# Queries and keys of the first batch entry: three rows to a partition, turned by products with the identity

## The chip, the cores and the metric

The kernel runs on one core of a Trainium2 chip. The metric is the device time of one launch in microseconds. The core has TensorE (PE; PEld is its loading of stationary operands), VectorE (DVE), ScalarE (ACT), GpSimd (POOL) and SyncE (SP), which issues all DMAs of this kernel. Each engine works through its own instructions in order.

## What is computed

Attention on q, k, v of shape (2, 8, 576, 64), followed by two feed-forward layers on the 1152 rows of 512. The change lies in the attention, of which this is the core:

```
q_d, k_d, v_d = means over groups of 4 rows            # 144 coarse rows
out_d   = softmax(scale * q_d @ k_d.T) @ v_d           # coarse attention
out_up  = each row of out_d repeated 4 times
scores  = scale * q @ k.T, masked to |i - j| < 4       # local attention
out     = out_up + softmax(scores) @ v
```

After it come a mixture of 8 experts, out = sum over e of P[:, e] * (relu(x @ w1[e]) @ w2[e]) with P from 8 rounds of row and column normalization, and softplus(x @ w_in) @ w_out.

## The kernel before

The attention is cut into eight units (`class Unit`): one unit is a pair of heads of one batch entry, and its `n` runs from 0 to 7, so units 0 to 3 are the first batch entry. A unit's q and k (576 rows of 64 values for each of two heads) are loaded by `load_qk` with four DMAs of 144 KB: queries in partitions 0 to 63, keys in 64 to 127; a partition holds row p of each of nine blocks of 64 rows. A DMA piece is one row, 256 bytes. Units 1 and 2 load into buffers of the expert weights (`qkw`), the others into one buffer `qk`.

`setup(g)`, called for g = 0, 1, 2, turns three of the nine blocks: three TensorE transposes of 128x128 write a PSUM bank `tb`, whose partitions are then the 64 values of head 0 and of head 1. From `tb` VectorE sums groups of four columns into `qkd` (L539), ScalarE copies the keys, scaled, into `kT` (L550), and the queries go to `fine`, one half by VectorE (L551), one by ScalarE (L552). After the third call VectorE scales the coarse queries into `flat` (L545). The layout of a bank is block, then query or key, then row.

`scores` makes four score blocks of a unit ("c" is the coarse one, 0 to 2 the local ones), the softmax runs on VectorE and ScalarE (small, sc, ex), `turn` transposes the weights (L609, L619), and `values` multiplies them with v (L630 coarse, L641 local; these write the lower and the upper 64 partitions in turn). `stir` (L479) issues products of the identity whose results nothing reads; they stand ahead of the scores and turns of units 0 to 3, and eight more at the very start. The values v come in `vw` and `vd`; GpSimd sums `vd` into `vs` (L559, L560). In the second half of the attention the first steps of the experts (L866, L954) are put between (`beside`), and expert weights are split into two parts (w1h, w1l, w2h, w2l, L274 to L314).

In the attention a scheduler at build time sets the order on each engine, from the dependencies and its own estimates; from the experts on, the order is written by hand (`Order`). At most eight DMAs are outstanding: each waits for the one eight places earlier.

Of the kernel before, what the change touches and what calls it, by code (L numbers as in the profile page):

```python
# [9 lines left out]
F32 = mybir.dt.float32  # L10
# [4 lines left out]
ALU = mybir.AluOpType  # L15
AX = mybir.AxisListType
# [4 lines left out]
def attention_moe_mlp(ctx: ExitStack, tc: tile.TileContext, q, k, v, w_gate, w1, w2, w_in, w_out, out):  # L21
    nc = tc.nc
    B, H, S, D = q.shape
# [3 lines left out]
    P = 128  # L27
    R = 4
    SD = S // R
    HC = SD // 2  # L30
    QT = 64
    NQ = S // QT
    NB = 3
    CT = SD // NB
    KW = QT + 2 * R
    KD = DM // P
    SCALE = 1.0 / float(D) ** 0.5
# [24 lines left out]
    rows = [ctx.enter_context(tc.tile_pool(name="rows0", bufs=len(TILES[0])))]  # L62
# [32 lines left out]
    ident = const.tile([P, P], F32, name="ident")  # L95
# [357 lines left out]
    ap = at.__enter__()  # L453
# [18 lines left out]
    fine = [ap.tile([P, NB, 2, QT], F32, bufs=1, name=f"fine{g}") for g in range(NB)]  # L472
# [11 lines left out]
    class Unit:  # L484
# [12 lines left out]
        def load_qk(self):  # L497
            b, h0 = self.b, 2 * self.u
            if self.n in (1, 2):
                qk = wp.tile([P, OPS, 2, P], F32R, tag="w1h" if self.n == 1 else "w1l", name="qkw").bitcast(F32)  # L500
                qk = qk.rearrange("p a k c -> p (a k c)")[:, : NQ * 2 * D]
                qk = qk.rearrange("p (t h d) -> p t h d", t=NQ, h=2)
            else:
                qk = ap.tile([P, NQ, 2, D], F32, tag="qk", bufs=1, name="qk")
            self.qk = qk
            for w, src in enumerate((q, k)):
                for hh in range(2):
                    nc.sync.dma_start(
                        qk[w * QT : (w + 1) * QT, :, hh], src[b, h0 + hh].rearrange("(t p) d -> p t d", p=QT)
                    )  # L510

        def load_v(self):
            b, h0 = self.b, 2 * self.u
# [11 lines left out]
        def setup(self, g):  # L525

            if g == 0:
                self.kT = ap.tile([P, NQ, QT], F32, tag="kT", name="kT")
                self.qkd = ap.tile([P, NQ, 2, QT // R], F32, tag="qkd", name="qkd")
            qkd = self.qkd  # L530
            tb = self.bank("tb", 1)
            tiles = slice(NB * g, NB * g + NB)
            for j in range(NB):
                nc.tensor.transpose(
                    tb[:, j * P : (j + 1) * P], self.qk[:, NB * g + j].rearrange("p h d -> p (h d)"), ident
                )
            tb = tb[:, : NB * P]
            tbv = tb.rearrange("x (t w p) -> x t w p", t=NB, w=2)
            nc.vector.tensor_reduce(  # L539
                qkd[:, tiles].rearrange("x t w g -> x (t w) g"),  # L540
                tb.rearrange("x (t g r) -> x t g r", g=QT // R, r=R), axis=AX.X, op=ALU.add,
            )
            for hh in range(2 if g == NB - 1 else 0):
                half = slice(hh * D, (hh + 1) * D)
                nc.vector.tensor_scalar(  # L545
                    self.flat[half, :, hh].rearrange("x i (j g) -> x i j g", j=NB),
                    qkd[half, :, 0].rearrange("x (i j) g -> x i j g", i=NB),
                    SCALE / (R * R), None, op0=ALU.mult,
                )
            nc.scalar.mul(self.kT[:, tiles], tbv[:, :, 1], SCALE)  # L550
            nc.vector.tensor_copy(fine[g][:D, :, 0], tbv[:D, :, 0])  # L551
            nc.scalar.copy(fine[g][D:, :, 1], tbv[D:, :, 0])  # L552
            if g:
                return
            vd = self.vd

            self.vs = vs = ap.tile([HC, 2, 2, D], F32, tag="vs", name="vs")
            for c in range(2):
                nc.gpsimd.tensor_tensor(vd[:, c, :, 0:2, :], vd[:, c, :, 0:2, :], vd[:, c, :, 2:4, :], op=ALU.add)  # L559
                nc.gpsimd.tensor_tensor(vs[:, c], vd[:, c, :, 0, :], vd[:, c, :, 1, :], op=ALU.add)  # L560
# [133 lines left out]
    def logits():  # L694
        lg = bank("y", "lg")
        lts = [
            lowp[0].tile([P, SUMS * P], U32, tag="cva", name="lts").bitcast(F32)[: 2 * E],
            pair("lts").rearrange("p a c -> p (a c)")[: 2 * E],
        ]

        def half(s, j):
            lt = bank("at", "lt")
            terms = [
                (i, w, kk, x[s]) for i, w in (((4, 1), (5, 2)), ((3, 0), (1, 1)))[j]
                for kk in range(2) for x in (xh, xl)
            ]
            for n, (i, w, kk, x) in enumerate(terms):
                nc.tensor.matmul(
                    lt[: 2 * E, : HALF[s]], wgs[:, w, kk, :], x[:, i, kk, :],
                    start=(n == 0), stop=(n == len(terms) - 1),  # L710
                )
            nc.scalar.copy(halves(s, lts[s])[j], lt[: 2 * E, : HALF[s]])

        def short(s, t):
            o = t * P - T0[s]
            nc.tensor.transpose(
                lg[:, 2 * t * E : 2 * (t + 1) * E], lts[s][:, o : o + P], ident[: 2 * E, : 2 * E]
            )

        def done():  # L720
            nc.vector.tensor_reduce(
                pr, lg[:, : 2 * NTT * E].rearrange("p (t w e) -> p t e w", w=2, e=E), axis=AX.X, op=ALU.add
            )
            nc.vector.tensor_reduce(m1, prf, axis=AX.X, op=ALU.max)

        return half, short, done
# [339 lines left out]
    for n in range(len(stream) + LAG + 1):  # L1066
        if n < len(stream):
            x, blk = stream[n]
            i, j = divmod(n, len(blocks))
# [24 lines left out]
        for lag, what in ((LAG, "turn"), (LAG + 1, "values")):  # L1094
            if 0 <= n - lag < len(stream):
                x, blk = stream[n - lag]
# [22 lines left out]
    half, short, done = logits()  # L1119
# [46 lines left out]
    with tc.manual_schedule(engines=engines):  # L1166
# [3 lines left out]
        for n in range(BESIDE, len(steps)):  # L1170
            if n == CV:
                converting.append(order_.add(conversions(), 2))
            e, g, s, p = steps[n]
# [9 lines left out]
            half = [i for i in range(len(ys)) if (i + 1) * P > HALF[s]]  # L1183
            half = half[1:] + half[:1] if HALF[s] % P else half
            tiles = half + [i for i in range(len(ys)) if i not in half]
# [55 lines left out]
```

## Time and profile before

| | us |
|---|---|
| median of 3 runs | 1068.11 (1066.86 to 1068.22) |
| profiled execution | 1065.88 |
| its span | 1064.0 |
| TensorE busy | 1044.2 (98%) |
| VectorE busy | 692.5 (65%) |
| ScalarE busy | 570.0 (54%) |
| GpSimd busy | 556.1 (52%) |

The profile covers one execution; its times count from the start of the span. Busy TensorE means that matmuls are in flight, not that it runs at its peak, and the stirring products count as busy. A row of the timeline merges like instructions that follow each other: start, time, engine, line, operation, output and inputs, count, and in brackets the idle time before it with what ended it. A float32 product that is not a transpose shows as two records.

### The profile page before, as it was taken

What the parts mean: (1) busy time and instruction counts of PE and PEld (TensorE: products, weight loads), DVE (VectorE), ACT (ScalarE), POOL (GpSimd) and SP (SyncE); (2) the same over time, 40 slices, a digit from 0 to 9 for tenths busy, and PEclk for the clock granted to TensorE, in tenths of its full rate; (3) what the DMA queues carried; (4) which work ended last, traced back from release to release, by engine and by line L of the source; (5) the groups of instructions that cost most, each with busy time, mean ns of one, the idle gap of its engine ahead of it and who ended that gap; (6) DMA issues with size and microseconds to landing.
All of it is one profiled execution on the core that took longest, in us unless ns stands there. A gap on an engine that the chain in (4) does not pass through costs nothing.

```text
span 1064.0 us, 17733 instructions
## 1 busy us (share of the span) xinstructions
PE 1044.2 (98%) x6417; PEld 925.7 (87%) x6417; DVE 692.5 (65%) x1416; ACT 570.0 (54%) x1479; POOL 556.1 (52%) x575
## 2 busy tenths in 40 slices
PE   7989999999999999999999999999999999999998
PEld 5778888898999989898998989899998999888897
DVE  4896666765656566566756665665664677876674
ACT  4887654435444444454444445444544667666664
POOL 3658433487556575555556666664574413222322
PEclk8999999999999999999999999999999999999999
DMA  9463201233333335243333333443334485533752
GB/s 175 131 136 84 85 21 41 61 94 114 95 115 90 99 94 154 80 128 114 117 114 94 101 108 94 118 126 100 119 99 140 147 295 211 217 149 129 262 202 80
DMA packets 135799, 131.22 MB, mean 123 GB/s; under 512 B 36000, under 2 KB 112032, under 8 KB 135712
## 3 DMA queue, kind: packets, MB, share of 16 engines
q1 hardware_dynamic: 135712, 130.10, 39.9%
q8 instruction: 50, 0.82, 0.3%
q14 instruction: 37, 0.30, 0.1%
HBM read 104.64 MB, written 25.43 MB: 122 GB/s over the span
## 4 chain that ended last, share of the span: by engine, by line
PE 83%; DVE 8%; ACT 5%; POOL 2%; DMA 1%; issue 1%; SPq 0%; ACTq 0%
PE yps L954 41%; PE m L866 37%; POOL ab L830 2%; DVE ab L833 1%; ACT one L828 1%; DVE ab L826 1%; PE sc L582 1%; DVE one L824 1%; DVE xl L439 1%; DVE c L885 1%; PE pv L641 1%; DMA raw<-in_moe_w 1%; ACT ab L815 1%; PE tp L619 1%; PE sc L569 1%
## 5 line engine op out<-in xcount | busy, mean ns | idle before, releaser
L866 PE MATMUL m<-xh,w1h 128*128 128x320 f32 (+1 forms) x1120 | 333.8, 298 | 3.5 <-ACT t L878 2.4
L866 PE MATMUL m<-xl,w1h 128*128 128x320 f32 (+1 forms) x1120 | 331.7, 296 | 1.1 <-DVE xl L439 1.1
L866 PE MATMUL m<-xh,w1l 128*128 128x320 f32 (+1 forms) x1120 | 331.6, 296 | 0.0
L866 PEld LDWEIGHTS m<-xh,w1h 128*128 128x128 f32 x1120 | 211.8, 189 | 20.1 <-ACT t L878 4.0
L866 PEld LDWEIGHTS m<-xl,w1h 128*128 128x128 f32 x1120 | 211.9, 189 | 14.4 <-DVE xl L439 1.5
L866 PEld LDWEIGHTS m<-xh,w1l 128*128 128x128 f32 x1120 | 211.8, 189 | 0.3 <-issue 0.2
L954 PE MATMUL yps<-w2h,hh 128*128 128x512 f32 x502 | 198.9, 396 | 0.0
L954 PE MATMUL yps<-w2l,hh 128*128 128x512 f32 x502 | 198.3, 395 | 0.0
L954 PE MATMUL yps<-w2h,hl 128*128 128x512 f32 x502 | 195.9, 390 | 0.0
L954 PE MATMUL yps<-w2h,h 128*128 128x512 f32 x436 | 152.8, 392 | 0.0
L293 POOL TENSOR_TENSOR w1l<-sums,w1h 128x512 fp32r<-128x512 f32 x72 | 99.5, 1394 | 90.9 <-ACT w1h L291 79.3
L885 DVE TENSOR_TENSOR c<-m,t 128x256 f32<-128x256 f32 (+1 forms) x160 | 72.8, 455 | 114.0 <-PE m L866 68.8
L314 POOL TENSOR_TENSOR w2l<-raw,w2h 128x512 fp32r<-128x512 f32 x72 | 98.8, 1391 | 60.0 <-ACT w2h L312 59.8
L803 ACT ACTIVATE hh<-c 128x256 fp32r<-128x256 f32 (+1 forms) x138 | 60.8, 444 | 127.7 <-DVE c L885 127.5
L830 POOL TENSOR_TENSOR ab<-one,ab 128x320 f32<-128x320 f32 (+1 forms) x64 | 55.3, 866 | 141.0 <-ACT one L828 140.9
L984 DVE SCALAR_TENSOR_TENSOR acc<-yps,pr,acc 128x512 f32<-128x512 f32 x117 | 87.2, 745 | 53.0 <-PE yps L954 52.4
L805 DVE SCALAR_TENSOR_TENSOR hl<-c,hh 128x256 fp32r<-128x256 f32 (+1 forms) x138 | 93.3, 679 | 31.7 <-ACT hh L803 30.1
L954 PEld LDWEIGHTS yps<-w2h,hl 128*128 128x128 f32 x502 | 94.4, 188 | 21.6 <-issue 0.2
L954 PEld LDWEIGHTS yps<-w2h,hh 128*128 128x128 f32 x502 | 94.7, 189 | 12.5 <-DVE small L589 0.2
L878 ACT COPY t<-m 128x256 f32<-128x256 f32 (+1 forms) x160 | 62.6, 398 | 77.9 <-PE m L866 77.7
L954 PEld LDWEIGHTS yps<-w2l,hh 128*128 128x128 f32 x502 | 94.8, 189 | 10.7
L954 PEld LDWEIGHTS yps<-w2h,h 128*128 128x128 f32 x436 | 82.1, 188 | 14.7
(141 smaller groups left out, 1647.2 us busy)
## 6 DMA issues: line engine op xcount, KB each, us to landing
raw<-in_moe_w SPq DMA_DIRECT2D x72, 256.0 KB
raw<-in_moe_w SPq DMA_DIRECT2D x36, 512.0 KB
w1h<-s_in SPq DMA_DIRECT2D x14, 896.0 KB
w1l<-s_in SPq DMA_DIRECT2D x14, 896.0 KB
raw<-in_moe_w_in SPq DMA_DIRECT2D x32, 256.0 KB
raw<-in_moe_w_out SPq DMA_DIRECT2D x16, 512.0 KB
w2l<-s_out SPq DMA_DIRECT2D x14, 512.0 KB
w2h<-s_out SPq DMA_DIRECT2D x14, 512.0 KB
```

The lines of the kernel that those rows point to most:

```text
L293: behind(chain, nc.gpsimd.tensor_tensor(lo[:, part], sums, hi[:, part].bitcast(F32), op=ALU.subtract))
L314: behind(chain, nc.gpsimd.tensor_tensor(lo[:, i], raw[:, i], hi[:, i].bitcast(F32), op=ALU.subtract))
L439: nc.vector.tensor_tensor(xl[s][:, i, kk], src, xh[s][:, i, kk].bitcast(F32), op=ALU.subtract)
L569: nc.tensor.matmul(sc[:rows, i * w : (i + 1) * w], self.flat[:, i].rearrange("x h q -> x (h q)"), self.qkd[:, :, 1], start=True, stop=True,)
L803: nc.scalar.activation(hh, c, AF.Relu)
L805: nc.vector.scalar_tensor_tensor(out=hl, in0=c, scalar=0.0, in1=hh.bitcast(F32), op0=ALU.max, op1=ALU.subtract)
L830: nc.gpsimd.tensor_tensor(ab, one, ab, op=ALU.subtract)
L866: nc.tensor.matmul(b[:, :h], x[:, i, kk, :], y[s][:, i, kk, :], start=(not more and n == 0), stop=(n == 5), skip_group_check=more,)
L878: nc.scalar.copy(t, b[:, :h])
L885: nc.vector.tensor_tensor(c, b[:, :h], t, op=ALU.add)
L954: nc.tensor.matmul(y, a[:, f, tok], b[:, f, :], start=(start and m == 0), stop=(stop and m == 5))
L984: nc.vector.scalar_tensor_tensor(out=acc[t], in0=y, scalar=pr[:, t, e : e + 1], in1=acc[t], op0=ALU.mult, op1=ALU.add,)
```

## The change

For units 0 to 3 (`thirds`) a partition now holds, in each third of a head's rows, three rows that follow each other (g, then p, then j), so a DMA piece is 768 bytes. Turning such a third by a transpose of whole blocks would leave the rows in the order j, p. So the turning of a third is six products of the loaded data (stationary, 64 columns: one head's row j) with the identity (moving, 128 columns): for each j one product for head 0, into partitions 0 to 63, and one for head 1, into 64 to 127, and each writes every third column of `tb`. A bank's layout is now query or key, then rows in order, for all units. Units 4 to 7 keep their loads and transposes, which write two pieces of 64 columns each. What reads `tb` changes its views, not its sizes; `qkd` is laid out by third, then query or key.

```diff
@@ -499,15 +499,22 @@
             if self.n in (1, 2):
                 qk = wp.tile([P, OPS, 2, P], F32R, tag="w1h" if self.n == 1 else "w1l", name="qkw").bitcast(F32)
                 qk = qk.rearrange("p a k c -> p (a k c)")[:, : NQ * 2 * D]
+            else:
+                qk = ap.tile([P, NQ * 2 * D], F32, tag="qk", bufs=1, name="qk")
+            self.thirds = self.n < 4
+            if self.thirds:
+                qk = qk.rearrange("p (g h j d) -> p g h j d", g=NB, h=2, j=NB)
+            else:
                 qk = qk.rearrange("p (t h d) -> p t h d", t=NQ, h=2)
-            else:
-                qk = ap.tile([P, NQ, 2, D], F32, tag="qk", bufs=1, name="qk")
             self.qk = qk
             for w, src in enumerate((q, k)):
                 for hh in range(2):
-                    nc.sync.dma_start(
-                        qk[w * QT : (w + 1) * QT, :, hh], src[b, h0 + hh].rearrange("(t p) d -> p t d", p=QT)
-                    )
+                    rows = src[b, h0 + hh]
+                    if self.thirds:
+                        rows = rows.rearrange("(g p j) d -> p g j d", g=NB, j=NB)
+                    else:
+                        rows = rows.rearrange("(t p) d -> p t d", p=QT)
+                    nc.sync.dma_start(qk[w * QT : (w + 1) * QT, :, hh], rows)
@@ -526,30 +533,35 @@
             if g == 0:
                 self.kT = ap.tile([P, NQ, QT], F32, tag="kT", name="kT")
-                self.qkd = ap.tile([P, NQ, 2, QT // R], F32, tag="qkd", name="qkd")
+                self.qkd = ap.tile([P, NB, 2, CT], F32, tag="qkd", name="qkd")
             qkd = self.qkd
             tb = self.bank("tb", 1)
             tiles = slice(NB * g, NB * g + NB)
+            tb = tb[:, : NB * P]
             for j in range(NB):
-                nc.tensor.transpose(
-                    tb[:, j * P : (j + 1) * P], self.qk[:, NB * g + j].rearrange("p h d -> p (h d)"), ident
-                )
-            tb = tb[:, : NB * P]
-            tbv = tb.rearrange("x (t w p) -> x t w p", t=NB, w=2)
+                if self.thirds:
+                    to = tb.rearrange("x (w p j) -> x w p j", w=2, j=NB)[:, :, :, j]
+                    for hh in range(2):
+                        nc.tensor.matmul(
+                            to[hh * D : (hh + 1) * D], self.qk[:, g, hh, j],
+                            ident.rearrange("k (w p) -> k w p", w=2), start=True, stop=True,
+                        )
+                else:
+                    to = tb.rearrange("x (w t p) -> x w t p", w=2, t=NB)[:, :, j]
+                    nc.tensor.transpose(to, self.qk[:, NB * g + j].rearrange("p h d -> p (h d)"), ident)
             nc.vector.tensor_reduce(
-                qkd[:, tiles].rearrange("x t w g -> x (t w) g"),
-                tb.rearrange("x (t g r) -> x t g r", g=QT // R, r=R), axis=AX.X, op=ALU.add,
+                qkd[:, g].rearrange("x w g -> x (w g)"),
+                tb.rearrange("x (g r) -> x g r", r=R), axis=AX.X, op=ALU.add,
             )
             for hh in range(2 if g == NB - 1 else 0):
                 half = slice(hh * D, (hh + 1) * D)
                 nc.vector.tensor_scalar(
-                    self.flat[half, :, hh].rearrange("x i (j g) -> x i j g", j=NB),
-                    qkd[half, :, 0].rearrange("x (i j) g -> x i j g", i=NB),
-                    SCALE / (R * R), None, op0=ALU.mult,
+                    self.flat[half, :, hh], qkd[half, :, 0], SCALE / (R * R), None, op0=ALU.mult,
                 )
-            nc.scalar.mul(self.kT[:, tiles], tbv[:, :, 1], SCALE)
-            nc.vector.tensor_copy(fine[g][:D, :, 0], tbv[:D, :, 0])
-            nc.scalar.copy(fine[g][D:, :, 1], tbv[D:, :, 0])
+            tbv = tb.rearrange("x (w t p) -> x w t p", w=2, p=QT)
+            nc.scalar.mul(self.kT[:, tiles], tbv[:, 1], SCALE)
+            nc.vector.tensor_copy(fine[g][:D, :, 0], tbv[:D, 0])
+            nc.scalar.copy(fine[g][D:, :, 1], tbv[D:, 0])
```

The scheduler also moves instructions. Line numbers of the changed kernel are 11 to 13 higher from here on (L534 becomes L545, L569 L581, L582 L594, L619 L631, L641 L653). On TensorE at the head, from the last mask product of the first scores (qk is unit 0's data and stands just before, qkw unit 1's), before:

```order
L576 MATMUL sc<-mask,identb 128x216
L534 MATMUL tb<-ident,qkw 128x128 x3
L582 MATMUL sc<-kT,fine_147 128x72 x3
L534 MATMUL tb<-ident,qkw 128x128 x3
L582 MATMUL sc<-kT,fine_148 128x72 x3
L479 LDWEIGHTS identb
L479 MATMUL tp<-identb 128x512
L569 MATMUL sc<-qkd,flat_150 96x144 x3
```

and in the changed kernel:

```order
L588 MATMUL sc<-mask,identb 128x216
L545 MATMUL tb<-ident,qkw 64x128 x6
L594 MATMUL sc<-kT,fine_147 128x72 x3
L545 MATMUL tb<-ident,qkw 64x128 x6
L581 MATMUL sc<-qkd,flat_150 96x144 x3
L594 MATMUL sc<-kT,fine_148 128x72 x3
L479 LDWEIGHTS identb
L479 MATMUL tp<-identb 128x512
```

The coarse scores of unit 0 (flat_150) moved ahead of its second local block and of a stirring product. On VectorE at the same place (flat_150 is unit 0's coarse queries; the copies fine_147 and fine_148 behind it are unit 1's), before:

```order
L545 TENSOR_SCALAR flat_150<-qkd 64x3x48 x2
L539 TENSOR_REDUCE qkd<-tb 128x96
L551 COPY fine_149<-tb 64x3x64
L551 COPY fine_147<-tb 64x3x64
L539 TENSOR_REDUCE qkd<-tb 128x96
L551 COPY fine_148<-tb 64x3x64
L589 TENSOR_REDUCE small<-sc 96x3
L589 TENSOR_REDUCE small<-sc 128x3 x2
```

and in the changed kernel:

```order
L558 TENSOR_SCALAR flat_150<-qkd 64x3x48 x2
L552 TENSOR_REDUCE qkd<-tb 128x96
L563 COPY fine_149<-tb 64x3x64
L563 COPY fine_147<-tb 64x3x64
L552 TENSOR_REDUCE qkd<-tb 128x96
L601 TENSOR_REDUCE small<-sc 96x3
L601 TENSOR_REDUCE small<-sc 128x3 x2
L563 COPY fine_148<-tb 64x3x64
```

The maxima of unit 0's scores (small) moved ahead of the copy for unit 1's second third. On TensorE where unit 2 (again qkw) is turned, before:

```order
L534 MATMUL tb<-ident,qkw 128x128 x5
L619 MATMUL tp<-ident,ex 72x128 x3
L479 LDWEIGHTS identb
L479 MATMUL sc<-identb 128x512
L576 LDWEIGHTS identb
L576 MATMUL sc<-mask,identb 128x216
L582 MATMUL sc<-kT,fine_148 128x72 x3
L534 MATMUL tb<-ident,qkw 128x128
L479 LDWEIGHTS identb
L479 MATMUL tp<-identb 128x512
L641 MATMUL pv<-et,vw 64x64 x6
```

and in the changed kernel:

```order
L545 MATMUL tb<-ident,qkw 64x128 x7
L631 MATMUL tp<-ident,ex 72x128
L653 MATMUL pv<-et,vw 64x64 x6
L631 MATMUL tp<-ident,ex 72x128 x2
L479 LDWEIGHTS identb
L479 MATMUL sc<-identb 128x512
L588 LDWEIGHTS identb
L588 MATMUL sc<-mask,identb 128x216
L594 MATMUL sc<-kT,fine_148 128x72 x3
L545 MATMUL tb<-ident,qkw 64x128 x5
```

The six transposes of the first two thirds became twelve products, split 7 and 5, and a block of values (pv) moved up between them.

## Rows read from the trace of the kernel before

**Rows 1.** The page's first line.

```profile
span 1064.0 us, 17733 instructions
```

**Rows 2.** Stretches: length, busy (count) PE PEld DVE ACT POOL, clock, DMA, GB/s.

```profile
13.70:16.70 3.00, 0.00 (x0) 0.00 (x0) 2.32 (x10) 2.71 (x19) 1.55 (x4) 0.93 1.37 138
16.70:23.10 6.40, 6.36 (x27) 5.01 (x28) 2.58 (x12) 2.69 (x11) 0.87 (x2) 0.50 1.17 173
23.10:34.60 11.50, 11.50 (x116) 9.15 (x115) 8.20 (x30) 8.87 (x40) 3.59 (x7) 1.00 0.56 144
34.60:46.20 11.60, 11.60 (x122) 9.14 (x120) 10.59 (x32) 11.35 (x51) 9.50 (x13) 1.00 0.51 119
46.20:60.00 13.80, 9.60 (x90) 7.78 (x90) 13.00 (x33) 9.94 (x39) 12.24 (x16) 0.90 0.83 183
60.00:75.00 15.00, 13.05 (x120) 10.59 (x119) 13.45 (x42) 12.59 (x54) 8.93 (x10) 0.98 0.46 127
75.00:140.00 65.00, 64.94 (x555) 55.58 (x554) 45.64 (x124) 46.38 (x164) 40.49 (x42) 1.00 0.30 78
140.00:1064.00 924.00, 917.37 (x5346) 822.50 (x5343) 590.91 (x1125) 470.81 (x1098) 472.20 (x461) 1.00 0.38 124
```

**Rows 3.** The chain of waits, 0 to 36 us: start, us, what.

```profile
5.58 4.03 DMA qkw<-in_k
...
12.46 0.35 DVE fine L551
12.82 0.62 DVE small L589
...
16.74 1.17 PE tp L609 x6
...
34.63 0.38 DVE small L589
```

**Rows 4.** Timeline of TensorE at the head.

```profile
5.33 1.16 PE L479 MATMUL sc<-identb 128*128 128x512 bf16 x3
6.50 1.18 PE L534 MATMUL tb<-ident,qk 128*128 128x128 f32 x9
7.51 0.35 PE L576 MATMUL sc<-mask,identb 128*128 128x216 bf16 x2
9.74 0.52 PE L534 MATMUL tb<-ident,qkw 128*128 128x128 f32 x3 [1.88 <-DMA qkw<-in_k]
...
16.74 1.17 PE L609 MATMUL tp<-ident,ex 96*72 96x96 f32 x6 [3.15 <-DVE ex L597]
```

**Rows 5.** Timeline of TensorE: ordinary float32 products, and what follows them.

```profile
27.65 0.57 PE L641 MATMUL pv<-et,vw 72*64 72x64 f32 x12
28.15 0.44 PE L609 MATMUL tp<-ident,ex 96*72 96x96 f32 x3
...
42.20 0.90 PE L569 MATMUL sc<-qkd,flat 128*96 128x144 f32 x6
43.03 0.72 PE L630 MATMUL pv<-etc,vs 72*64 72x144 f32 x8
43.67 0.52 PE L619 MATMUL tp<-ident,ex 128*72 128x128 f32 x3
```

**Rows 6.** Timeline of VectorE.

```profile
46.46 0.38 DVE L589 TENSOR_REDUCE small<-sc 128x3 f32<-128x216 f32 x1 [0.89 <-PE sc L582]
...
48.22 2.25 DVE L435 TENSOR_TENSOR xf<-xf 128x256 f32<-128x256 f32 x1
...
65.10 0.41 DVE L435 TENSOR_TENSOR x<-xf 128x256 f32<-128x256 f32 x1
```

**Rows 7.** Columns as in rows 2: first loads; a stretch of larger packets.

```profile
2.00:10.00 8.00, 6.10 (x25) 2.85 (x26) 2.52 (x7) 1.54 (x6) 4.67 (x16) 1.00 1.01 183
24.50:27.00 2.50, 2.50 (x23) 2.30 (x22) 1.70 (x6) 1.48 (x10) 0.00 (x0) 1.00 1.05 327
```

## Prediction, made before the changed kernel ran

> **What bounds the kernel now.** I read the page's span first [rows 1], then the busy times by stretch [rows 2], then the chain of waits over the first 36 us [rows 3], then the timelines of TensorE and VectorE at the places that the change touches [rows 4 to 6], and last the DMA rates [rows 7]. The profiled execution is 1065.88 us, 1064.0 us of it span and 1.88 us around it.
>
> From 75 us to the end TensorE is the bound: 64.94 of 65 us and then 917.37 of 924 us busy [rows 2]. The change touches nothing there, so what it does is the shift with which the work at 75 us arrives. [...] Up to 16.7 us the chain is made of latencies: issuing and landing of the loads of units 0 and 1 (the last one 4.03 us from issue to landing), then VectorE and ScalarE on the first softmax [rows 3]. TensorE waits 1.88 us for unit 1's keys, and 3.15 us for the first normalized scores [rows 4]. [...] From 34.6 to 46.2 us TensorE (11.60 of 11.60), ScalarE (11.35) and VectorE (10.59) are all full; from 46.2 to 75 us VectorE leads, and TensorE idles 4.2 + 1.95 = 6.15 us [rows 2].
>
> **What one unit's turning costs.** Nine transposes begin at 6.50 and the next instruction at 7.51: 0.112 us each [rows 4]. Now there are 18 ordinary float32 products, each with 64 stationary and 128 moving columns, in pairs that write the lower and upper half of the partitions. The nearest rows are L630: four products of 144 columns into such halves, shown as eight records, take 43.67 - 43.03 = 0.64 us [rows 5], 0.16 us each, by columns 0.142 us for 128. So a unit takes 18 x 0.142 = 2.56 us in place of 1.01: **+1.55 us**. From below: L569, 96 stationary columns, takes (43.03 - 42.20)/3 = 0.277 us for 144 columns [rows 5], 0.246 for 128; two exactly side by side cost 0.123 each, a unit +1.2 us. From above, as long as pairs overlap: L641, 64 columns, (28.15 - 27.65)/6 = 0.083 [rows 5], doubled 0.167, a unit +2.0 us. I take L630, the form nearest to the new one. No row has an output that writes every third column; its price is a rival below.
>
> The trace has a float32 product at 0.246 us for 128 columns against a transpose at 0.112 [rows 4, 5]: 2.2 times. [...]
>
> **The head, up to 16.7 us.** The gain is the load. Eight DMAs of 144 KB carry units 0 and 1, 1.18 MB, at 183 GB/s with 256-byte pieces [rows 7], which is 6.4 us. Pieces of 768 bytes go somewhere between that rate and the 327 GB/s of a stretch whose packets are larger [rows 7], which would be 3.6 us; so unit 1's keys land 0 to 2.8 us earlier. I take a landing before 9.1 us. Unit 0 gains nothing from its earlier landing: TensorE is in the stirring products (L479) until 6.50 [rows 4]. Its 18 products then run to 6.50 + 2.56 = 9.06, two mask products (7.86 - 7.51 = 0.35, where 7.86 is the 9.74 less 1.88 of waiting) to 9.41. Unit 1's first third starts at 9.41 instead of 9.74, but takes 0.85 instead of 0.33 us: it is ready at 10.26 against 10.07. The wait is replaced by work, +0.2. The new order gives something back: VectorE now does the first three maxima ahead of a copy that stood before them, 12.82 - 12.46 in its queue, 0.36 us [rows 3], and TensorE brings the coarse scores ahead of one block. With a second slow third (+0.5) partly beside VectorE, I get the first softmax at **-0.1 us**, bounds -0.8 (cheap pairs, the copy's 0.36 and the earlier start whole) and +0.6 (dear pairs, no landing gained). Unit 1's last third lies before the wait of 3.15 us and costs nothing; without that cover it would be +0.5.
>
> **Units 2 and 3.** Their loads were already early: both are turned after 25 us, behind the busy TensorE. So there the change is pure added work in a full queue: unit 2 in the stretch to 34.6 us, unit 3 in the next. 2 x 1.55 = **+3.1 us** (2.4 to 4.0). In the next stretch VectorE is nearly full too, but at 46.46 it has just waited 0.89 us for TensorE's scores [rows 6], so the delay passes.
>
> **What takes it back.** From 46.2 to 75 us TensorE idles 6.15 us, and VectorE loses time that has nothing to do with TensorE's lateness: a subtraction of 128x256 takes 2.25 us at 48.22, and 0.41 at 65.10 [rows 6]. Work that arrives later fits partly into these holes. I take half of the 3.1: **-1.6 us** (0 to -3.1).
>
> **Moved at no price.** The scheduler reorders all engines through the attention; VectorE's and ScalarE's instructions stay the same in size. On SyncE unit 1's value load now stands ahead of the last key load, unit 2's ahead of the first expert's weights; on GpSimd one part of a weight goes behind a value sum. I price this at nothing, since the chain to 46 us runs through neither queue; what it can move is a stall such as the one at 48.22, 2.25 - 0.41 = 1.8 us either way [rows 6]. Batch 1's transposes keep count and size.
>
> **Sum:** -0.1 + 3.1 - 1.6 = +1.4 us: 1065.88 + 1.4 = 1067.3 for an execution like the profiled one. That one is 2.23 us under the median of 1068.11, so the forecast for a median is 1069.5 us.
>
> **Rivals.**
> - *Nothing is taken back.* VectorE and ScalarE wait for TensorE as at 46.46 and carry the delay whole to 75 us: -0.1 + 3.1 = +3.0, up to +4.6 with the upper bounds; 1071.1 us. It decides once TensorE is the last to arrive at 46 us. For it: TensorE full from 16.7 to 46.2; against it: the holes of 6.15 us. Slower; chance 0.20.
> - *The products are dear.* If pairs don't run side by side (the columns a third apart in PSUM), a product costs 0.246 us, a unit +3.4: head +2.2, two units +6.9, less 1.6, is +7.5 us, 1075.6. Decides from about 0.17 us per product. Against it: L630 and L641 both cost less than alone. [...] Slower; chance 0.10.
> - *The clock stays up.* The granted clock fell to half for 16.7 to 23.1 us after TensorE had done nothing from 13.7 to 16.7 [rows 2]. With longer products before it and an earlier softmax that gap shrinks to perhaps 2.3 us. If the clock holds, 6.36 us of products at half speed become 3.2: -3.2, sum -1.8; and if the holes swallow all of the added work too, -3.4, 1064.7 us. Against it: most of the gap remains. Chance 0.30, of which 0.23 ends faster (with the reordered stalls of up to 1.8 us helping) and 0.07 within the bound.
> - *The load gains nothing* (unit 1 still lands at 9.7): that is the +0.6 of the head, inside the forecast.
>
> **How the numbers follow.** The forecast's own case, part of the delay taken back, has 0.40, all within 0.2% (2.1 us, about what a measurement of this kernel can tell from no change). Faster 0.23; same 0.40 + 0.07 = 0.47; slower 0.20 + 0.10 = 0.30. The range goes from the clock case with everything swallowed, 1064.7, to the delay carried whole with the upper bounds, 1068.11 + 4.6 = 1072.7; the dear products are left out.
>
> **What would show it.** Unit 0's 18 products should span 2.2 to 3.0 us from 6.50; TensorE's wait for unit 1's keys should be gone; the first transposes of normalized scores (16.74) should come between 15.9 and 17.3; the point at 34.6 should lie 1 to 2 us later, that at 46.2 some 3 us, and from 75 us on every row +1.4. A unit over 3.0 us, or a granted clock of 1.00 between 16.7 and 23.1, would make the forecast wrong, in opposite directions.

## The result, and the profile after

The changed kernel takes 1073.24 us (median of 6 runs, 1071.89 to 1073.80), the kernel before, in the same comparison, 1067.35 (6 runs, 1066.32 to 1068.22): a ratio of 1.0054, 95% interval 1.0042 to 1.0065. It is slower by 5.9 us. The forecast was 1069.5 with a range to 1072.7, so the time lies outside the range, and "slower" had 0.30.

The profiled execution is 1073.38 us, of which 1071.5 are span: 7.5 more than in [rows 1]. The stretches, cut as in [rows 2] (length, busy time and count of PE, PEld, DVE, ACT, POOL, granted clock, DMA share, GB/s):

```profile
13.70:16.70 3.00, 1.82 (x17) 0.87 (x16) 2.39 (x9) 2.69 (x17) 0.58 (x2) 1.00 0.58 151
16.70:23.10 6.40, 5.64 (x33) 4.43 (x34) 2.97 (x13) 3.16 (x15) 2.23 (x4) 0.73 0.69 190
...
46.20:60.00 13.80, 11.39 (x107) 9.20 (x106) 12.31 (x36) 11.63 (x46) 9.86 (x12) 0.88 0.67 173
60.00:75.00 15.00, 8.72 (x78) 7.39 (x79) 12.76 (x23) 7.37 (x34) 9.80 (x12) 0.77 0.37 92
75.00:140.00 65.00, 63.69 (x567) 55.18 (x568) 46.14 (x139) 47.27 (x176) 38.29 (x41) 1.00 0.37 96
```

The row from 60 us stands out. From 60 to 75 us TensorE is busy 8.72 us, where it was 13.05, and ScalarE 7.37, where it was 12.59, while VectorE counts as busy for 12.76 us with 23 instructions in place of 42: few, and long. To place it, follow two groups that mark the flow from unit 3 to unit 4 through TensorE: the coarse values of unit 3 and the coarse scores of unit 4. Timeline of TensorE, before:

```profile
43.03 0.72 PE L630 MATMUL pv<-etc,vs 72*64 72x144 f32 x8
...
55.22 0.72 PE L630 MATMUL pv<-etc,vs 72*64 72x144 f32 x8
...
57.63 1.73 PE L569 MATMUL sc<-qkd,flat 128*96 128x144 f32 x6 [1.69 <-ACT et L620]
```

and after (the coarse values of unit 2 stand first in both):

```profile
47.30 0.72 PE L642 MATMUL pv<-etc,vs 72*64 72x144 f32 x8
...
58.06 0.72 PE L642 MATMUL pv<-etc,vs 72*64 72x144 f32 x8
66.15 1.72 PE L581 MATMUL sc<-qkd,flat 128*96 128x144 f32 x6 [7.38 <-DVE flat L558]
```

Unit 2's values come 4.27 us late, unit 3's 2.84, so some delay had been taken back. Then the next step, 2.41 us before, takes 8.09: **5.7 us are lost in one place**, while TensorE waits 7.38 us for `flat`, the scaled coarse queries of unit 4. The timeline of VectorE there, and that of GpSimd:

```profile
60.06 5.94 DVE L558 TENSOR_SCALAR flat<-qkd 64x144 f32<-64x144 f32 x2
```

```profile
59.82 1.04 POOL L572 TENSOR_TENSOR vs<-vd 72x128 f32<-72x128 f32 x2
60.83 1.26 POOL L276 TENSOR_TENSOR w1l<-raw,w1h 128x512 fp32r<-128x512 f32 x1
62.05 1.26 POOL L314 TENSOR_TENSOR w2l<-raw,w2h 128x512 fp32r<-128x512 f32 x1
63.27 0.72 POOL L242 TENSOR_TENSOR sums<-raw 128x256 f32<-128x256 f32 x1
63.95 1.26 POOL L314 TENSOR_TENSOR w2l<-raw,w2h 128x512 fp32r<-128x512 f32 x1
65.17 0.72 POOL L242 TENSOR_TENSOR sums<-raw 128x256 f32<-128x256 f32 x1
```

The chain of waits splits the pair:

```profile
60.13 3.28 DVE flat L558
...
63.43 2.59 DVE flat L558
```

The two scalings have 144 elements per partition each. All sixteen of them in the kernel, by line (minimum, median, maximum in ns), before and after:

```profile
L545 DVE TENSOR_SCALAR flat<-qkd x16: 282/297/300, 9.0 to 110.9; 64x144 f32<-64x144 f32 x16
```

```profile
L558 DVE TENSOR_SCALAR flat<-qkd x16: 240/256/3355, 10.6 to 117.4; 64x144 f32<-64x144 f32 x16
```

Size and count are the same, but it runs in another way: a seventh faster as a rule, and 3.4 us at worst, where GpSimd works without a pause beside it. What differs is only the views (read from the two kernels; the rows show no more than 64x144). Before, the scaling read nine pieces of 16 columns and wrote three rows of three pieces; after, both sides are three pieces of 48.

After the change a pair takes 0.51 us at 10.60, where GpSimd is idle (for 4.88 us, until it begins its sums at 12.05), and 5.94 beside the run of sums and splits above. By the median one scaling went from 0.297 to 0.256 us. Why the new views should make it wait for GpSimd, no row shows; whether they do is what the runs below decide.

### The profile page after: what moved, and what is told of

Same layout as the page of the kernel before. It is cut to its first block, busy times and chain, and to the rows that moved or that the text cites. A ratio compares the mean times of both kernels' runs of the same rounds, so it can differ in the third digit from the quotient of the medians.

```text
span 1071.5 us, 17947 instructions
## 1 busy us (share of the span) xinstructions
PE 1051.1 (98%) x6525; PEld 931.3 (87%) x6525; DVE 693.0 (65%) x1416; ACT 570.0 (53%) x1479; POOL 555.9 (52%) x575
## 4 chain that ended last, share of the span: by engine, by line
PE 84%; DVE 9%; ACT 4%; POOL 2%; issue 1%; ACTq 0%; DVEq 0%; POOLq 0%
PE yps L966 40%; PE m L878 36%; POOL ab L842 2%; DVE ab L845 1%; ACT one L840 1%; PE sc L594 1%; DVE ab L838 1%; DVE xl L439 1%; DVE one L836 1%; PE tb L545 1%; DVE c L897 1%; DVE flat L558 1%; PE tp L631 1%; PE pv L653 1%; PE sc L581 1%
```

## The experiments

Three theories could be told apart. *Form*: the scaling waits for GpSimd because of its new views. *Order*: the scheduler's new order makes the loss, and `flat` only happened to stand there. *Products*: the dearer turning is carried to the end. The first four kernels vary the code and let the scheduler set the order again; in what was expected of them, theory A is *form* and theory B *products*.

**e1_flat_apart**: all of the change, but the coarse rows and their scaling as before.

```diff
-                self.qkd = ap.tile([P, NB, 2, CT], F32, tag="qkd", name="qkd")
+                self.qkd = ap.tile([P, NQ, 2, QT // R], F32, tag="qkd", name="qkd")
-                qkd[:, g].rearrange("x w g -> x (w g)"),
-                tb.rearrange("x (g r) -> x g r", r=R), axis=AX.X, op=ALU.add,
+                qkd[:, tiles].rearrange("x t w g -> x w t g"),
+                tb.rearrange("x (w t g r) -> x w t g r", w=2, t=NB, r=R), axis=AX.X, op=ALU.add,
...
-                    self.flat[half, :, hh], qkd[half, :, 0], SCALE / (R * R), None, op0=ALU.mult,
+                    self.flat[half, :, hh].rearrange("x i (j g) -> x i j g", j=NB),
+                    qkd[half, :, 0].rearrange("x (i j) g -> x i j g", i=NB),
+                    SCALE / (R * R), None, op0=ALU.mult,
```

> The changed kernel, but the coarse sums qkd keep the layout of the kernel before, so that the scaling into flat reads nine pieces of 16 instead of three of 48; loads and products stay as changed. Theory A (the contiguous form of that scaling waits for GpSimd: 5.94 us for two of them at 60 us in the changed kernel): no scaling lasts over 0.35 us, TensorE has no stall of 5 us near 60 us, and the time is 1068.5 to 1071 (the lag of the added products alone, which stood at +2.8 us just ahead of the stall). Theory B (the added products cost the 6 us, and the wait on the scaling only stands where they would have been waited for anyway): 1072 to 1074.

Measured: 1070.74 us (10 runs), ratio 1.0035 (1.0020 to 1.0050). It lies in the range of theory A. Every scaling takes 0.28 to 0.30 us again; by the medians 2 us or a little more of the 5.9 are gone (0.54% against 0.35%), but the two intervals overlap.

**e2_layout_only**: the new layouts with no new loads or products.

```diff
-            self.thirds = self.n < 4
+            self.thirds = False
```

> The changed kernel with no unit loaded in threes: loads of 256-byte pieces and transposes for all units, but the new layout of the banks, of qkd and the contiguous scaling into flat. Theory A: scalings of 0.24 to 0.26 us where GpSimd is idle, and over 1 us wherever a run of GpSimd instructions meets them; if the pair of unit 4 falls into the run near 55 to 65 us, 1070 to 1073, with no lag before it. Theory B: 1067.4 within 1 us, as the kernel before.

Measured: 1075.89 us (4 runs), ratio 1.0079 (1.0056 to 1.0101): outside what either theory gave, and by the medians slower than the whole change.

**e5_before_flat**: the kernel before with only `qkd` laid out by third, so that the scaling is contiguous.

```diff
-                self.qkd = ap.tile([P, NQ, 2, QT // R], F32, tag="qkd", name="qkd")
+                self.qkd = ap.tile([P, NB, 2, CT], F32, tag="qkd", name="qkd")
-                qkd[:, tiles].rearrange("x t w g -> x (t w) g"),
-                tb.rearrange("x (t g r) -> x t g r", g=QT // R, r=R), axis=AX.X, op=ALU.add,
+                qkd[:, g].rearrange("x w (t c) -> x t w c", t=NB),
+                tb.rearrange("x (t w c r) -> x t w c r", t=NB, w=2, r=R), axis=AX.X, op=ALU.add,
...
-                    self.flat[half, :, hh].rearrange("x i (j g) -> x i j g", j=NB),
-                    qkd[half, :, 0].rearrange("x (i j) g -> x i j g", i=NB),
-                    SCALE / (R * R), None, op0=ALU.mult,
+                    self.flat[half, :, hh], qkd[half, :, 0], SCALE / (R * R), None, op0=ALU.mult,
```

> The kernel before, with only qkd laid out by third and the scaling into flat contiguous (three pieces of 48 on both sides). Loads, transposes and banks as before. Theory A: scalings of 0.24 to 0.26 us alone and over 1 us beside a run of GpSimd; slower by what the pairs wait, 0 to 6 us, and most of it in one pair between 55 and 66 us if it falls into the run of GpSimd there. Theory B: 1067.4 within 1 us, no scaling over 0.35 us.

Measured: 1074.23 us (4 runs), ratio 1.0066 (1.0045 to 1.0086): above both ranges again. These two have no new load and no new product, and lose at least as much as the change itself (the intervals overlap). But in their traces a scaling takes 0.88 us at most, less than the "over 1 us" of theory A. VectorE and GpSimd in e5_before_flat:

```profile
49.53 0.36 DVE L658 TENSOR_TENSOR xf<-pv,xc 128x192 f32<-128x192 f32 x1 [4.76 <-PE pv L639]
...
61.25 5.25 DVE L439 TENSOR_TENSOR xl<-xf,xh 128x256 fp32r<-128x256 f32 x2
```

```profile
45.62 0.72 POOL L557 TENSOR_TENSOR vd<-vd 72x256 f32<-72x256 f32 x1 [1.49 <-DMA vd<-in_v]
...
61.63 1.26 POOL L314 TENSOR_TENSOR w2l<-raw,w2h 128x512 fp32r<-128x512 f32 x1
62.86 1.27 POOL L276 TENSOR_TENSOR w1l<-raw,w1h 128x512 fp32r<-128x512 f32 x1
64.09 1.26 POOL L314 TENSOR_TENSOR w2l<-raw,w2h 128x512 fp32r<-128x512 f32 x1
```

Here two subtractions, in the same form in all kernels, take 5.25 us beside three weight splits in a row on GpSimd, which the kernel before never has in a row there (in e2_layout_only such a pair takes 6.26 us, beside the same three); and at 49.5 VectorE has stood idle for 4.76 us; the chain of waits leads from there back to the load of values for which GpSimd waits at 45.62. So a loss of that size doesn't need a slow scaling, and e2 and e5 decide nothing between form and order, since both edits also moved instructions on every engine.

**e4_unit1_apart**: e1_flat_apart with the new load and products in unit 1 only.

```diff
-            self.thirds = self.n < 4
+            self.thirds = self.n == 1
```

> Loads in threes and products for unit 1 alone, the only unit whose data TensorE waited for, and the scaling into flat as before. Theory A: no long scaling; the wait of 1.9 us for unit 1's keys is mostly gone, a gain of 0.3 to 1.2 us at the first softmax, and 1066.2 to 1067.3 in all. Theory B: 1.1 us of added products less that gain, 1067 to 1068.

Measured: 1064.87 us (10 runs), ratio 0.9981 (0.9966 to 0.9996): faster than the kernel before, and below what either theory gave. More on it below.

**Order and form apart.** The next kernels hold the order. A chain of dependencies that makes nothing wait but the issue runs through all instructions of each engine, from the first load to the experts' hand-written order, and sets them in a given kernel's order (`PLACES` holds it as numbers; where code and order are of different kernels, a third's six products stand for its three transposes):

```diff
+        for _ in range(count):
+            place += int.from_bytes(raw[at : at + 2], "big") - 8192
+            at += 2
+            for ins in items[place]:
+                if last is not None:
+                    tc.add_manual_dep(
+                        ins, last.name,
+                        mybir.DependencyInfo(mybir.DependencyClass.NoSync, mybir.DependencyReason.DATA),
...
+    pin(tc, nc.cur_bb.bb.instructions[begun:], joined)
```

**x1_after_old_order**: the changed kernel's code in the order of before.

> The changed kernel with every engine's instructions, from the first load to the experts' hand-written order, held in the order of the kernel before (a chain of dependencies without waits; the six products of a third stand where its three transposes stood). Theory 'order': the 5.9 us of the changed kernel come mostly from the new order, which bunches GpSimd's instructions and lets VectorE wait for them at 58 to 66 us; here only the added TensorE work is left, 1066 to 1069.5 us, no wait of VectorE over 2.5 us. Theory 'form': the scaling of the coarse queries, contiguous on both sides now, waits for GpSimd wherever it stands; 1071 to 1075 us, with the waits in the rows of flat.

**x2_before_new_order**: the code of before in the changed kernel's order.

> The kernel before, held in the order of the changed kernel on all engines; nothing of the change itself is in it. Theory 'order': as slow as the changed kernel less the added TensorE work, 1069.5 to 1073 us, with a wait of VectorE of 3 us or more at 58 to 66 us in whatever instruction stands there. Theory 'form': the scaling is in its old form and does not wait; 1065 to 1068 us.

**x3_layout_old_order**: the code of e5_before_flat in the order of before.

> The kernel before with the coarse rows laid out by third, so that the scaling of the coarse queries is contiguous on both sides, held in the order of the kernel before. Without the hold this edit gave 1074.2. Theory 'order': 1066 to 1068 us. Theory 'form': 1070 to 1075 us.

**x5_flat_apart_old_order**: the code of e1_flat_apart in the order of before.

> The changed loads and products, but the coarse rows and their scaling as in the kernel before (nine pieces), held in the order of the kernel before. Theory 'order': within 1 us of the changed kernel in the old order, 1066 to 1069.5 us. Theory 'form': 1066 to 1070 us, and 3 us or more under the changed kernel in the old order.

**x8_flat_apart_new_order**: the same code in the changed kernel's order.

> The changed loads and products, the coarse rows and their scaling as in the kernel before (nine pieces), held in the order of the changed kernel: all of the change but the contiguous scaling. Theory 'form': 2.5 to 4 us under the changed kernel's 1073.2, 1069.0 to 1071 us, and no scaling over 0.35 us. Theory 'order': within 1 us of the changed kernel, 1072.2 to 1074 us.

Measured, with the kernels they are corners of (each ratio is to the kernel before in the same comparison; the 29 runs are those beside x1, x2, x3 and x5):

| products | scaling | order | kernel | us | ratio to before |
|---|---|---|---|---|---|
| no | nine pieces | old | before | 1067.36 (29 runs) | 1 |
| no | contiguous | old | x3 | 1072.22 (6) | 1.0040 (1.0026 to 1.0055) |
| yes | nine pieces | old | x5 | 1070.19 (12) | 1.0015 (1.0000 to 1.0031) |
| yes | contiguous | old | x1 | 1072.81 (12) | 1.0042 (1.0028 to 1.0055) |
| no | nine pieces | new | x2 | 1069.10 (12) | 1.0009 (0.9996 to 1.0022) |
| yes | nine pieces | new | x8 | 1069.68 (12) | 1.0023 (1.0009 to 1.0038) |
| yes | contiguous | new | after | 1073.24 (6) | 1.0054 (1.0042 to 1.0065) |

Read in pairs, the contiguous scaling costs 0.40% alone, 0.27% beside the products (x1 less x5) and 0.31% in the new order (after less x8): 2.9 to 4.3 us, and by the intervals each of the three is clear of zero. The products with their loads cost 0.15% (x5), 0.02% (x1 less x3) and 0.14% (x8 less x2), 0.2 to 1.6 us. The new order costs 0.09% (x2), 0.08% (x8 less x5), 0.12% (after less x1), about 1 us. None of these six can be told from nothing. So *form* is the largest part, in either order: x1, x3 and x8 lie where it had put them and outside what *order* gave for them. *Order* falls as the main cause. *Form* alone isn't all either: x2 (1069.10) is above its 1065 to 1068 and just below the other theory's 1069.5, and x5 is just above the 1070 that *form* allowed and 2.6 us under x1, not 3. The wait of VectorE of 3 us or more that *order* expected in x2 isn't there: its longest instruction from 58 to 66 us is a subtraction of 2.41 us.

The rows show the same. x8 differs from the changed kernel only in the scaling, with the layout of `qkd`, and in being held to that kernel's order. Its VectorE at the scaling for unit 4:

```profile
59.05 0.60 DVE L610 TENSOR_SCALAR flat<-qkd 64x144 f32<-64x144 f32 x2
```

GpSimd has the same run of sums and splits beside it, the pair takes 0.60 us instead of 5.94, and the scores of unit 4 begin 2.36 us after the coarse values of unit 3 instead of 8.09. But the 5.7 us lost in that one place are not the price of the scaling. From the coarse values of unit 3 to those of unit 4 TensorE takes 17.22 us before, 21.67 in the changed kernel, and 20.65 in x8: most of the loss comes a little later there, without a slow scaling. The price is what the medians say.

VectorE at the same place in x3, and GpSimd beside it:

```profile
58.37 2.27 DVE L596 TENSOR_SCALAR flat<-qkd 64x144 f32<-64x144 f32 x2
...
61.18 2.22 DVE L488 TENSOR_TENSOR xl<-xf,xh 128x256 fp32r<-128x256 f32 x1
```

```profile
58.44 0.86 POOL L609 TENSOR_TENSOR vs<-vd 72x128 f32<-72x128 f32 x2 [0.27 <-PE pv L679]
59.26 1.26 POOL L363 TENSOR_TENSOR w2l<-raw,w2h 128x512 fp32r<-128x512 f32 x1
...
61.17 1.26 POOL L363 TENSOR_TENSOR w2l<-raw,w2h 128x512 fp32r<-128x512 f32 x1
```

and VectorE in the kernel before, in the same order:

```profile
56.88 0.60 DVE L545 TENSOR_SCALAR flat<-qkd 64x144 f32<-64x144 f32 x2
...
58.02 1.17 DVE L439 TENSOR_TENSOR xl<-xf,xh 128x256 fp32r<-128x256 f32 x1
```

The pair takes 2.27 us instead of 0.60, until the weight split has ended, and the subtraction behind it meets the next split and takes 2.22 instead of 1.17. TensorE waits 2.45 us for `flat` in x3; the kernel before waits 1.69 there, for ScalarE. What follows is paid at a lower clock. In x3 the granted clock is at the lower level, 0.50, from 56 to 72 us, behind a stretch in which TensorE was busy 2.25 of 4 us:

```profile
52.00:56.00 4.00, 2.25 (x10) 1.51 (x10) 4.00 (x13) 2.62 (x13) 2.83 (x4) 0.64 1.04 265
56.00:60.00 4.00, 2.18 (x12) 1.50 (x11) 3.99 (x8) 3.79 (x10) 3.65 (x5) 0.50 1.20 146
...
64.00:68.00 4.00, 4.00 (x28) 3.35 (x26) 1.60 (x6) 3.22 (x14) 2.61 (x4) 0.50 0.32 113
68.00:72.00 4.00, 4.00 (x26) 3.58 (x26) 2.73 (x8) 2.16 (x11) 1.18 (x1) 0.50 0.00 0
```

In x1, where the pair takes 2.26 us and TensorE waits the same 2.45, it is back at full clock from 64 us on:

```profile
60.00:64.00 4.00, 4.00 (x20) 3.54 (x19) 3.39 (x5) 1.09 (x4) 4.00 (x6) 0.54 0.53 157
64.00:68.00 4.00, 3.90 (x48) 3.19 (x47) 2.98 (x10) 3.85 (x21) 1.57 (x3) 1.00 0.05 18
```

On VectorE 1.67 and 1.05 us are lost in x3, 2.7 together, and x3 loses 4.3 us by its ratio. The two traces point to the clock for the rest. From the coarse values of unit 3 to those of unit 4 TensorE takes 17.22 us before, 18.61 in x1 and 21.21 in x3: the wait is the same, and 2.6 us more are lost where TensorE works on at half the clock. These are single executions, that of x1 the fastest of its twelve (1068.96 us, median 1072.81). Why the clock stays low in one and not in the other isn't shown, and the lower level comes without a slow scaling too: the scores at 57.63 in the kernel before take 1.73 us, as long as the 1.72 of those at 66.15 in the changed kernel (the group at 42.20 in [rows 5] took 0.90), and x2, x5 and x8 have 0.50 to 0.59 in 68 to 76 us.

**Is it GpSimd?** So far GpSimd only stands beside the wait. **x6_layout_short_gpsimd** and **x7_before_short_gpsimd** take it away: x3 and the kernel before, in the old order, with the two weight splits next to the scaling cut from 512 columns to 32.

```diff
-        weights.setdefault(f, {})[1] = hi, lo
+        weights.setdefault(f, {})[1] = hi, hi if f == 1 else lo
-            behind(chain, nc.gpsimd.tensor_tensor(lo[:, i], raw[:, i], hi[:, i].bitcast(F32), op=ALU.subtract))
+            cut = slice(0, 32 if f == 1 else DM)
+            behind(chain, nc.gpsimd.tensor_tensor(lo[:, i, cut], raw[:, i, cut], hi[:, i, cut].bitcast(F32), op=ALU.subtract))
```

> The layout-only kernel in the order of before (which gave 1072.2), with two instructions of GpSimd cut from 512 to 32 columns: the two halves of w2l of the second fetched weight, which stood beside the scaling of the coarse queries at 57 to 61 us; the experts read w2h in their place, so the result is not the reference's. Same instructions in the same order otherwise. If the scaling waits for GpSimd: its pair at 57 to 58 us takes at most 1.2 us instead of 2.27 (only the sums of values, 0.86 us, still stand beside it), and the kernel ends at most 2.5 us above the kernel before with the same cut. If the contiguous form is slow for another reason: the pair stays at 2.2 us.

> The kernel before with the same two instructions of GpSimd cut to 32 columns (the experts read w2h in their place, so the result is not the reference's), in its own order: the control for the run above. Theory 'form': the pair of scalings stays at 0.60 us; the subtractions beside the cut instructions, 1.17 and 1.11 us before, get shorter; 1065 to 1067.5 us. Theory 'order': the same.

Measured: x6 1068.62 us (10 runs), ratio 1.0014 (1.0001 to 1.0026); x7 1067.06 (10 runs), 1.0001 (0.9989 to 1.0013). With two instructions of GpSimd cut short, the price of the contiguous scaling falls from 0.40% to 0.13%; for the kernel before, the same cut is worth nothing. In x6, VectorE and GpSimd:

```profile
57.73 0.92 DVE L597 TENSOR_SCALAR flat<-qkd 64x144 f32<-64x144 f32 x2
...
59.20 0.55 DVE L489 TENSOR_TENSOR xl<-xf,xh 128x256 fp32r<-128x256 f32 x1
```

```profile
57.49 1.04 POOL L610 TENSOR_TENSOR vs<-vd 72x128 f32<-72x128 f32 x2
58.53 0.25 POOL L364 TENSOR_TENSOR w2l<-raw,w2h 128x32 fp32r<-128x32 f32 x1
```

The scaling now waits only for the sums of values, which end at 58.53, as it does at 58.65, and from the coarse values of unit 3 to those of unit 4 it is 17.72 us, against 17.20 in x7. The cut also frees the subtraction behind the scaling (0.55 us instead of 2.22), so their shares aren't told apart. With this the cause is shown from both sides. The contiguous scaling hardly waits once the splits are short (x6), and in nine pieces it doesn't wait at all, as in x8 and as all sixteen show in x5, which has every other part of the change, by line:

```profile
L610 DVE TENSOR_SCALAR flat<-qkd x16: 283/297/301, 10.1 to 115.4; 64x144 f32<-64x144 f32 x16
```

**e4_again**: the version with unit 1 alone, a second time.

> The new load and the products in unit 1 alone, the coarse rows as in the kernel before: a second measurement of the version that gave a ratio of 0.9981. Its gain is unit 1's keys, which no longer keep TensorE waiting 1.88 us, less 1.2 us of dearer turning: 0.5 to 2 us under the kernel before, 1065 to 1066.5 us.

Measured: 1064.58 us (12 runs), ratio 0.9976 (0.9965 to 0.9986), a little below what was expected. By the two ratios it is 2.0 and 2.6 us under the kernel before, the fastest of all. Its head in the timeline of TensorE:

```profile
9.08 1.32 PE L545 MATMUL tb<-ident,qkw 128*64 128x128 f32 x12 [0.72 <-DMA qkw<-in_k]
...
17.25 0.69 PE L623 MATMUL tp<-ident,ex 96*72 96x96 f32 x6 [2.08 <-DVE ex L611]
```

Unit 1's keys hold TensorE up for 0.72 us instead of the 1.88 of [rows 4], but the first normalized scores are turned at 17.25 (at 16.70 in its first profile), no earlier than the 16.74 before. It gets ahead behind that, where the clock is higher: the next transposes (L619 before, at 19.53) begin at 18.74 and 19.32. In both of its profiles the clock in 16.7 to 23.1 us is 0.73, where [rows 2] has 0.50, with 0.92 and 1.47 us of products in the three microseconds before, where there were none. x3 and x7, which turn everything as before, show 0.73 there too in their one profile, so that this is where the gain comes from is likely and not shown.

## Why the prediction was wrong, step by step

**Moved at no price: this step failed.** It says "VectorE's and ScalarE's instructions stay the same in size" and prices the rest at nothing, within 1.8 us. Counts and sizes did stay; the views of one instruction changed, and with them whether it waits for GpSimd. That is 2.9 to 4.3 of the 5.9 us, by the table. I had the wait before me. Beside the subtraction that takes 2.25 us from 48.22 on [rows 6], GpSimd in the kernel before has two splits in a row:

```profile
47.69 1.27 POOL L314 TENSOR_TENSOR w2l<-raw,w2h 128x512 fp32r<-128x512 f32 x1
48.93 1.26 POOL L293 TENSOR_TENSOR w1l<-sums,w1h 128x512 fp32r<-128x512 f32 x1
```

I took this for a stall that moves by 1.8 us at most, and used it as a hole that swallows delay instead of asking which instructions can fall into one. The other half of the step, the new order, is worth about 1 us, inside its 1.8.

**What one unit's turning costs: right, a little dear.** Six products of a third take from 9.88 to 10.68 us, 0.133 each, where 0.142 was taken:

```profile
6.74 2.92 PE L545 MATMUL tb<-ident,qk 128*64 128x128 f32 x36
9.59 0.36 PE L588 MATMUL sc<-mask,identb 128*128 128x216 bf16 x2
9.88 0.88 PE L545 MATMUL tb<-ident,qkw 128*64 128x128 f32 x12
10.68 0.89 PE L594 MATMUL sc<-kT,fine 128*128 128x72 f32 x6
```

At 0.133 a product, where 0.246 was worked out from L569 for one alone, pairs run side by side, and writing every third column has no price that shows beside the 0.142 from L630. The rival of dear products (0.246) is out. Only unit 0's 18 products, at the very start, need 2.85 us, 0.158 each.

**The head: +0.7 instead of -0.1.** The wait for unit 1's keys is gone, as said. But "Unit 1's last third lies before the wait of 3.15 us and costs nothing" was wrong: it now ends at 15.17, and its sums and scaling stand on VectorE ahead of unit 0's normalization. The chain of waits after:

```profile
14.34 0.83 PE tb L545 x12
...
15.19 0.57 DVE qkd L552
...
16.12 0.26 DVE flat L558
...
16.41 0.17 DVE small L607
```

The first normalized scores are turned at 17.46 (16.74 in [rows 4]), just above the term's upper bound of +0.6; the price for a lost cover, +0.5, was in the text, but not in these bounds. It is one execution: the two profiles of the version with unit 1 alone differ by 0.55 us at this point.

**Units 2 and 3, and what takes it back: about right in size.** 4.27 us late at unit 2's coarse values and 2.84 at unit 3's, so 1.4 was given back, where 1.6 was taken; less the head's 0.7, the two units have added 3.6 us, where 3.1 was taken. The kernels with every part of the forecast and without the contiguous scaling end near the +1.4 of the forecast and the +3.0 of its first rival, or above: +1.6 us (0 to 3.3) in x5, +2.5 (1.0 to 4.1) in x8, and +3.7 (2.1 to 5.3) in e1, with an order of its own.

**The clock.** It did stay up longer: 0.73 in 16.7 to 23.1 us, with 1.82 us of products before it where there were none. But the lower level came back behind the wait for `flat` (0.77 from 60 to 75 us, 0.98 in [rows 2]). That the wait brought it isn't shown: x8, without it, has 0.79 there.

## What to carry to other kernels

An edit that "only changes the view" of a VectorE instruction can change how it runs: here a scaling went from 0.297 to 0.256 us by the median, and from 0.300 to 3.36 at the longest. Compare its duration before and after, and look at what GpSimd does beside it. The faster form of a 0.3 us instruction was worth nothing here, where it waited beside GpSimd's splits of 1.26 us, and it cost TensorE, which stood waiting 7.38 us for the result. Don't take the length of a stall for its price: of the 5.7 us lost in one place, the pair with the same order (the changed kernel and x8) puts 3.3 on the scaling. Where a scheduler sets the order, hold the order fixed before judging an edit: the same edit lost 0.66% with a new order (e5) and 0.40% in the old one (x3), by medians whose intervals overlap.

## What the runs showed of the hardware

- The wait is not for one instruction. In the changed kernel the first scaling begins at 60.13 and ends at 63.41, with two sums of values and two weight splits on GpSimd in between, one right behind the other, the second split until 63.31. The second scaling goes from 63.43 to 66.02, through the rest of a sum, the next split and another sum, which ends at 65.89. Why each ends there, and not at the boundaries of GpSimd at 60.86, 62.09, 63.99 and 65.21, the rows don't tell.
- VectorE's subtractions of 128x256 (L435, L439) take longer beside GpSimd too, in the kernel before as well: 0.41 us at 67.38, while GpSimd is idle from 66.65 to 68.20, 1.17 beside a split (at 58.02), 2.25 beside two [rows 6], and a pair 5.25 us in e5_before_flat, beside three.
- Float32 products with 64 stationary columns, in pairs into the lower and the upper half of the partitions, took 0.133 us each for 128 columns (six from 9.88 to 10.68), with an output that writes every third column, and 0.158 each in unit 0.
